# Cached attention decode with a gate: 112-partition weights, ten heads of wo behind the last values, three heads' products moved, a bf16 gate product

## The chip, the cores and the metric

The kernel runs on one core of a Trainium2 chip. The metric is device time in microseconds (us) of the whole launch, the median of three runs. The profile covers the span from the first to the last instruction, which is about 2 us shorter than the device time (2513.1 against 2514.9 us in the profiled run). Five engines matter here: TensorE (PE), VectorE (DVE), ScalarE (ACT), GpSimd (POOL) and SyncE (SP, which only issues transfers), and beside them 16 DMA engines that bring data from HBM into SBUF.

## What is computed

One token is decoded. Its normalised input asks 16 heads of cached keys and values (65,536 positions of 256 numbers each, bf16), and the attention's output is multiplied with a gate that two dense layers make.

```python
x = A_x                                   # 1 x 1 x 448, bf16
xn = _layernorm(x, axis=-1)
q = (xn @ wq)                             # 448 -> 16 heads x 256
scores = einsum("bhqd,bhkd->bhqk", q, k_cache) * (256 ** -0.5)
p = softmax(scores)
o = einsum("bhqk,bhkd->bhqd", p, v_cache) # 16 heads, 65536 keys, 256
s = o.reshape(1, 1, 16 * 256) @ wo        # 4096 -> 448
g = silu(silu(xn @ w1) @ w2)              # 448 -> 1792 -> 448
out = x + s * g
```

Keys and values are 2 x 16 x 65,536 x 256 x 2 bytes, 1,074 MB of the 1,084 MB that the kernel reads. The rest is w1, w2, wq and wo.

## The kernel before: the parts that matter

A head is cut into 4 blocks, so there are 64 blocks of keys and 64 of values. A block is 128 partitions x 128 keys x 256 numbers, 64 KB to a partition. Three buffers `R[0]`, `R[1]`, `R[2]` of that size take keys and values in turn. VectorE and ScalarE share the products of query and keys, TensorE multiplies the softmax's weights with the values (a matmul of 512 columns for two keys), and after the last block the heads' outputs are multiplied with wo ("project", a matmul of 448 columns for half a head).

The first layers' weights lie in `R[2]` until they are used. 448 rows are 3.5 times 128, so each weight comes in two transfers: three rows to a partition, and the last 64 rows cut in halves.

```python
def load_rows(T, M, w, s):
    sp.dma_start(out=T[:, 0 : DF * w],
        in_=M[0 : DF * P].rearrange("(p c) n -> p (c n)", c=DF)).then_inc(s, 16)
    sp.dma_start(out=T[:, DF * w : DF * w + w // 2],
        in_=M[DF * P : D].rearrange("r (z n) -> (r z) n", z=2)).then_inc(s, 16)
# ... the start
    act.dma_start(out=x_f[0:1, :], in_=A_x[0, 0:1, :]).then_inc(dl["x"], 16)
    load_rows(w1_t, B_w1, F, dl["w1"])
    load_rows(wq_t, A_wq, HD, dl["wq"])
    load_keys(R[0], block(Kd, 0), 0, SUB, kl[0])
    # ... w2, the rest of the first key block, the second key block
```

At the end the last values `Vl` come in eight pieces (`vz`, in keys), and wo in pieces of heads (`pieces`). Heads 0 to 2 of wo (`wo_p`, `NPRE = 3`) are loaded early, after the first value block.

```python
    vn = cuts(0, 32, 64, 96, 128)                      # the last but one value block
    vz = cuts(0, 16, 40, 64, 80, 96, 112, 120, 128)    # the last value block
    nz = 2
    pieces = cuts(NPRE, 9, 11, 13, 15, 16)             # wo
# ... the order of the last transfers
    for (k0, k1), w in zip(vn, nl):
        load_keys(R[2], Vn, k0, k1, w)
    take(sp, vf[1])
    for (k0, k1), w in zip(vz[:nz], zl[:nz]):
        load_keys(R[1], Vl, k0, k1, w)
    take(sp, kf[0])
    load_wo(0)
    for (k0, k1), w in zip(vz[nz:], zl[nz:]):
        load_keys(R[1], Vl, k0, k1, w)
    for p in range(1, len(pieces)):
        load_wo(p)
```

TensorE's order at the end, with what ScalarE and VectorE do between (`keys` waits for each piece and multiplies it; `pe_rows` and `pe_bcast` spread a block's maximum; `act_softmax` makes the weights, which `take(pe, pv)` waits for; `pe_turn` turns a block's output):

```python
    keys(psO, 2, 2, vn, nl, 3, 4, False, od)
    act_out(); act_row(LAST - 1)
    take(pe, pv)
    keys(psO2, 0, 1, vz, zl, 0, nz, True)
    need("pe", t_o)
    pe.wait_ge(wp, 16);    project(0, NPRE)
    pe.wait_ge(wl[0], 16); project(*pieces[0])
    pe_turn()
    # ... the third piece, with pe_rows and pe_bcast inside it
    act_softmax(LAST + 1, PV[0][:, HK:KB], HK, KB)
    t_g = silu(g_t, ps_y, g_e, t_y)
    act_out(psO2)
    take(pe, pv)
    t15 = pe_sums(ps_m[:, 0:NL], N1, NENT)
    keys(psO, 0, 1, vz, zl, nz + 1, nz + 2, True)
    pe_turn()
    # ... VectorE: shares and weights of the last head
    keys(psO, 0, 1, vz, zl, nz + 2, len(vz), False, od)
    act_out()
    pe.wait_ge(wl[1], 16); project(*pieces[1])
    t = pe_turn(tok=True)
    # ... VectorE: the last head's output
    for p in range(2, len(pieces) - 1):
        pe.wait_ge(wl[p], 16); project(*pieces[p])
    pe.wait_ge(wl[len(pieces) - 1], 16)
    t = mark("pe", project(H1, H))
    t = mark("dve", dve.tensor_tensor(out=g_t, in0=ps_ao, in1=g_t, op=ALU.mult))
    t = mark("dve", dve.tensor_tensor(out=x_f[0:1, :], in0=g_t, in1=x_f[0:1, :], op=ALU.add))
    sp.dma_start(out=out[0, 0:1, :], in_=x_f[0:1, :]).then_inc(dl["out"], 16)
```

`g_t` and `ps_ao` are fp32, `x_f` is bf16; `ps_ao` lies in PSUM.

Of the kernel before, what the change touches and what calls it, by code (L numbers as in the profile page):

```python
# [14 lines left out]
KB = 128  # L15
# [9 lines left out]
def kernel(  # L25
# [30 lines left out]
    NSTEP = KB // SUB  # L56
    DF = D // P
    assert D == DF * P + P // 2
    HP = H // 2
    DX = DF + 2  # L60
    FC = F // P
# [18 lines left out]
    S = pool.tile([P, KB], fp32, name="S")  # L80
    S2 = pool.tile([P, KB], fp32, name="S2")
    PVV = pool.tile([P, NR * KB], bf16, name="PV")
# [4 lines left out]

    wo_p = pool.tile([P, NPRE, 2 * D], bf16, name="wo_p")
    hist = pool.tile([P, 2 + NENT, 4], fp32, name="hist")
# [6 lines left out]
    sml = pool.tile([P, 16], fp32, name="sml")  # L96
    xnT = pool.tile([P, DX], bf16, name="xnT")
    h1e = pool.tile([P, FC], fp32, name="h1e")
    h1s = pool.tile([P, FC], bf16, name="h1s")
    negM = pool.tile([P, H], fp32, name="negM")  # L100
    cf = pool.tile([P, NENT], fp32, name="cf")
    wgt = pool.tile([P, NENT], fp32, name="wgt")
    tot = pool.tile([P, H], fp32, name="tot")
    part = pool.tile([P, 2, NENT], fp32, name="part")
    OT32 = pool.tile([P, 2, H], fp32, name="OT32")
    OT = pool.tile([P, 2, H], bf16, name="OT")
# [5 lines left out]

    def rest(n0, n):
        return R[2][:, n0 : n0 + n], n0 + n

    wq_t, n = rest(0, DF * HD + HD // 2)
    Z, n = rest(n, DX * HP * HP)
    w1_t, n = rest(n, DF * F + F // 2)
    w2_t, n = rest(n, FC * D)
    xn, n = rest(n, D)  # L120
    xz, n = rest(n, 2 * P)
    h1r, n = rest(n, 2 * F)
    assert n <= KW
    h1r = h1r[0:1, :].bitcast(fp32)
    xn, xz = xn[0:1, :], xz[0:1, :].rearrange("o (z n) -> o z n", z=2)

# [11 lines left out]
    psO2, ps_qh = bank[4][0:2, :], bank[3][0:HP, :]  # L138
    ps_xt, ps_h = bank[2][:, 0:DX], bank[7][:, 0:FC]
    ps_z = bank[6][0:1, D : D + 1]  # L140
# [8 lines left out]
    def mark(e, ins):  # L149
        count[e] += 1  # L150
        ins.then_inc(line[e], 1)
        return (e, count[e])

    def need(e, *toks):
        for p, c in toks:
            if seen.get((e, p), 0) < c:
                eng[e].wait_ge(line[p], c)
                seen[(e, p)] = c
# [4 lines left out]
    def take(e, s, k=1):  # L163
        e.wait_ge(s, k).then_inc(s, -k)  # L164
# [17 lines left out]
    def cuts(*c):  # L182
        return tuple(zip(c[:-1], c[1:]))

    vn = cuts(0, 32, 64, 96, 128)
    vz = cuts(0, 16, 40, 64, 80, 96, 112, 120, 128)
    nz = 2
    nl = [kl[2], kq[2], kh[2], vl[2]]
    zl = [kl[1], kq[1], kh[1], vl[1], vf[2], kf[1], kf[2], sem("zl")]
    pieces = cuts(NPRE, 9, 11, 13, 15, 16)  # L190
    wl = [vf[0], vf[1], vh[2]] + [sem(f"wl{t}") for t in range(3, len(pieces))]
# [28 lines left out]

    def load_rows(T, M, w, s):
        sp.dma_start(
            out=T[:, 0 : DF * w], in_=M[0 : DF * P].rearrange("(p c) n -> p (c n)", c=DF)
        ).then_inc(s, 16)
        sp.dma_start(
            out=T[:, DF * w : DF * w + w // 2],
            in_=M[DF * P : D].rearrange("r (z n) -> (r z) n", z=2),
        ).then_inc(s, 16)

# [107 lines left out]
    def act_out(po=psO):  # L337
        take(act, od)
        act.copy(out=O[:, :], in_=po).then_inc(oc, 1)  # L339

    def act_row(e):
        take(act, ho)
        return act.copy(out=hist[:, at(e + 2), 2:4].rearrange("p o s -> p (o s)"), in_=ps_t)
# [197 lines left out]
    with tc.tile_critical(sync_engine=ET.Pool, no_gpsimd_drain=True):  # L541


        act.dma_start(out=x_f[0:1, :], in_=A_x[0, 0:1, :]).then_inc(dl["x"], 16)
        load_rows(w1_t, B_w1, F, dl["w1"])
        load_rows(wq_t, A_wq, HD, dl["wq"])
        load_keys(R[0], block(Kd, 0), 0, SUB, kl[0])
# [11 lines left out]
        gp.memset(ones_row[:], 1.0)  # L559
        gp.memset(xz, 0.0)  # L560
        gp.memset(ident[:], 0.0)
# [29 lines left out]
        ))  # L591
        need("dve", t, g_c)
        for z in range(2):
            t5 = mark("dve", dve.tensor_copy(
                out=xz[0:1, z, :].rearrange("o (r y) -> o y r", y=2)[:, z, :],
                in_=xn[0:1, DF * P : D],
            ))

        xn_c = xn[0:1, 0 : DF * P].rearrange("o (p c) -> o c p", c=DF)
        need("pe", t5, g_c)  # L600
        for c in range(DX):
            ins = pe.matmul(
                ps_xt[:, c : c + 1],
                lhsT=xn_c[0:1, c, :] if c < DF else xz[0:1, c - DF, :],
                rhs=ones_row[0:1, 0:1],
                start=True,
                stop=True,
            )
# [5 lines left out]
        t_z = mark("dve", dve.tensor_copy(  # L614
            out=Z.rearrange("p (c n) -> p c n", c=DX)[:, :, 0 : (HP - 1) * (HP + 1) + 1 : HP + 1],
            in_=xnT[:, :, None].to_broadcast([P, DX, HP]),
        ))


        def rows(T, w, n0, n1):  # L620
            z, o = (n0 * 2) // w, DF * w
            return [(T[:, c * w + n0 : c * w + n1], c) for c in range(DF)] + [
                (T[:, o + n0 - z * (w // 2) : o + n1 - z * (w // 2)], DF + z)
            ]


        need("pe", t7)
        take(pe, dl["w1"], 32)
        FQ = F // 4
        for g, b in enumerate((0, 1, 5, 6)):  # L630
            for r, (w, c) in enumerate(rows(w1_t, F, g * FQ, (g + 1) * FQ)):
                ins = pe.matmul(
                    bank[b][0:1, 0:FQ],
                    lhsT=xnT[:, c : c + 1],
                    rhs=w,
                    start=(r == 0),
                    stop=(r == DF),
                )
            t = mark("pe", ins)
            need("act", t)  # L640
            t = mark("act", act.copy(out=h1r[:, g * FQ : (g + 1) * FQ], in_=bank[b][0:1, 0:FQ]))
# [21 lines left out]

        take(pe, dl["wq"], 32)
        for r, (w, c) in enumerate(rows(wq_t, HD, 0, Dh)):
            ins = pe.matmul(
                ps_q,
                lhsT=xnT[:, c : c + 1].to_broadcast([P, P]),
                rhs=w,
                start=(r == 0),  # L670
                stop=(r == DF),
            )
        ins.then_inc(qr, 1)
        need("pe", t_z)
        for j in range(HP):
            for r, (w, c) in enumerate(rows(wq_t, HD, j * 2 * Dh, (j + 1) * 2 * Dh)):
                ins = pe.matmul(
                    ps_qh,
                    lhsT=Z[:, (c * HP + j) * HP : (c * HP + j + 1) * HP],
                    rhs=w,  # L680
                    start=(j == 0 and r == 0),
                    stop=(j == HP - 1 and r == DF),
                )
# [173 lines left out]
        def keys(po, t, s, cut, sems, a, b, start, done=None):  # L857
            for n in range(a, b):
                (k0, k1), last = cut[n], n == b - 1
                pe.wait_ge(sems[n], 16)  # L860
                pe_keys(po, t, s, k0, k1, start and n == a, last and done is not None,
                        done if last else None)
# [5 lines left out]
        keys(psO, 2, 2, vn, nl, 3, 4, False, od)  # L868
        act_out()
        act_row(LAST - 1)  # L870


        take(pe, pv)
        keys(psO2, 0, 1, vz, zl, 0, nz, True)
        need("pe", t_o)
        pe.wait_ge(wp, 16)
        project(0, NPRE)
        pe.wait_ge(wl[0], 16)
        project(*pieces[0])
        pe_turn()  # L880
        (k0, k1) = vz[nz]
        assert k1 == HK
        pe.wait_ge(zl[nz], 16)
        pe_keys(psO2, 0, 1, k0, k0 + 8, False, False)
        pe_rows()
        pe_keys(psO2, 0, 1, k0 + 8, k0 + 16, False, False)
        pe_bcast()
        pe_keys(psO2, 0, 1, k0 + 16, k1, False, True, od)
        act_softmax(LAST + 1, PV[0][:, HK:KB], HK, KB)
        t_g = silu(g_t, ps_y, g_e, t_y)  # L890
        act_out(psO2)
        take(pe, pv)
        t15 = pe_sums(ps_m[:, 0:NL], N1, NENT)
        keys(psO, 0, 1, vz, zl, nz + 1, nz + 2, True)
        pe_turn()
        t = mark("dve", shares(N1, NENT, H1, H))
# [8 lines left out]
        outputs(N1, NENT - 1, H1, H, NL - 1)  # L905
        keys(psO, 0, 1, vz, zl, nz + 2, len(vz), False, od)
        act_out()
# [12 lines left out]
        for p in range(2, len(pieces) - 1):  # L920
# [5 lines left out]
        need("dve", t, t_g)  # L926
        t = mark("dve", dve.tensor_tensor(out=g_t, in0=ps_ao, in1=g_t, op=ALU.mult))  # L927
        need("dve", t)
        t = mark("dve", dve.tensor_tensor(  # L929
            out=x_f[0:1, :], in0=g_t, in1=x_f[0:1, :], op=ALU.add  # L930
        ))
        need("sp", t)
# [31 lines left out]
```

## Time and profile before

| what | value |
|---|---|
| time, three runs | 2515.05, 2515.18, 2515.19 us |
| span of the profiled run | 2513.1 us |
| read from HBM | 1084.29 MB, 431 GB/s over the span |
| VectorE busy | 2174.9 us (87%) |
| ScalarE busy | 1930.3 us (77%) |
| TensorE matmul busy | 1148.4 us (46%) |

How to read it: an engine's busy time is the sum of its instructions; a wait is idle time of an engine with what ended it. For the 16 DMA engines the profile has a mean busy share for each stretch, and the trace a record of every packet (its start, duration and size) and of every step by which a transfer's semaphore rises. A transfer of this kernel has landed for its reader when the slowest of its 16 engines is done.

### The profile page before, as it was taken

The numbers are of one execution on the slowest core, as the hardware profiler recorded it, in microseconds if no ns is written. First come the engines' busy times: TensorE is split into PE (matmuls) and PEld (weight loads), VectorE is DVE, ScalarE is ACT, GpSimd is POOL, SyncE is SP. The second block draws the span as 40 slices with busy tenths as digits, with TensorE's granted clock in tenths as the row PEclk, the third lists the DMA queues.
The fourth block names the chain that finished last, engine by engine and source line by source line (L and its number), as shares of the span: only waits on it lengthen the run. The fifth ranks groups of instructions, "written<-read, shape, count | busy, mean of one in ns | idle before, by whom it ended". The sixth has DMA issues, their size and how long they took to land. (4 is left out here: it accounts for less than half of the span.)

```text
span 2513.1 us, 29999 instructions
## 1 busy us (share of the span) xinstructions
PE 1148.4 (46%) x4738; PEld 436.0 (17%) x4738; DVE 2174.9 (87%) x1565; ACT 1930.3 (77%) x9556; POOL 1.9 (0%) x14
## 2 busy tenths in 40 slices
PE   3353543534535445345354353443544534535457
PEld 1121211211112112111121121111211111112123
DVE  6979889889898898898988988989889889898897
ACT  5868778778787787787877877878778778787786
POOL 0000000000000000000000000000000000000000
PEclk7676766767667677677676776776767767677679
DMA  9999999999999999999999999999999999999999
GB/s 426 421 442 434 434 434 433 434 433 432 433 434 434 432 432 432 432 434 433 433 434 434 434 434 434 434 433 434 434 434 434 434 434 434 434 434 434 434 426 375
DMA packets 23464, 1084.37 MB, mean 431 GB/s; under 512 B 2466, under 2 KB 4644, under 8 KB 5028
## 3 DMA queue, kind: packets, MB, share of 16 engines
q1 hardware_dynamic: 23458, 1084.30, 99.9%
q8 instruction: 4, 0.07, 0.0%
q10 hardware_dynamic: 2, 0.00, 0.0%
HBM read 1084.29 MB, written 0.00 MB: 431 GB/s over the span
## 5 line engine op out<-in xcount | busy, mean ns | idle before, releaser
L313 ACT ACTIVATE R<-R x4608 | 1839.0, 400 | 368.6 <-ACTq L164 368.6
L250 DVE TENSOR_TENSOR R<-R,qcur 128x4608 bf16<-128x4608 bf16 (+1 forms) x512 | 1131.1, 2220 | 248.7 <-DVEq L164 248.6
L348 PE MATMUL bank<-R,PV 128*2 128x512 bf16 x4096 | 1028.8, 418 | 18.7 <-PEq L164 6.0
L296 DVE TENSOR_REDUCE S<-R 128x13 f32<-128x3328 bf16 (+1 forms) x256 | 926.0, 3617 | 0.0
L313 ACT ACTIVATION_READ_ACCUMULATOR R<-R x4608 | 858.2, 186 | 0.0
L348 PEld LDWEIGHTS bank<-R,PV 128*2 128x2 bf16 x4096 | 365.0, 90 | 652.6 <-issue 212.5
L360 PE MATMUL bank<-ident,rmax 128*1 128x128 bf16 x65 | 17.0, 262 | 931.4 <-PEq L164 931.4
L377 PE MATMUL bank<-eye,O 2*128 2x2 f32 x264 | 40.1, 253 | 378.7 <-PEq L164 378.7
L360 PEld LDWEIGHTS bank<-ident,rmax 128*1 128x1 bf16 x65 | 5.1, 79 | 936.0 <-issue 935.9
L326 ACT ACTIVATE hist<-bank 128x1 f32 (+1 forms) x65 | 11.1, 171 | 158.0 <-ACTq L164 158.0
L284 DVE CUSTOM_DVE_ANT_0 R<-R,qcur 128x256 bf16<-128x256 bf16 x252 | 105.5, 419 | 0.0
L377 PEld LDWEIGHTS bank<-eye,O 2*128 2x128 f32 x264 | 36.3, 206 | 396.4 <-issue 396.4
L232 DVE TENSOR_REDUCE gmax<-bank 1x1 bf16<-1x128 f32 x65 | 18.3, 281 | 37.1 <-DVEq L164 37.1
L339 ACT COPY O<-bank 2x512 f32<-2x512 f32 x67 | 37.5, 559 | 8.2 <-ACTq L164 8.2
L271 DVE CAST qcur<-bank 128x256 bf16<-128x256 f32 x64 | 27.2, 425 | 16.0 <-DVEq L164 15.9
L328 ACT ACTIVATE PV<-S,hist 128x128 f32 (+1 forms) x65 | 26.0, 400 | 14.7 <-ACTq L164 14.5
L391 PE MATMUL bank<-q,ident 8*128 (+1 forms) x63 | 24.3, 386 | 7.8 <-issue 1.4
L243 DVE COPY S<-S 128x128 f32<-128x128 f32 (+1 forms) x65 | 14.7, 226 | 11.7 <-DVEq L164 2.5
L284 DVE DVE_READ_ACCUMULATOR2_ANT S<- 128x1 f32 x252 | 20.9, 83 | 0.0
L244 DVE TENSOR_REDUCE rmax<-S 128x1 bf16<-128x128 f32 (+1 forms) x65 | 18.2, 279 | 0.0
L366 PE MATMUL bank<-gmax,ones_row 1*128 1x1 bf16 x65 | 10.4, 159 | 4.4 <-PEq L164 0.6
L328 ACT ACTIVATION_READ_ACCUMULATOR PV<-S,hist (+1 forms) x65 | 12.1, 186 | 0.0
(72 smaller groups left out, 98.7 us busy)
## 6 DMA issues: line engine op xcount, KB each, us to landing
R<-in_A_k_cache_dram SPq DMA_DIRECT2D x7, 4096.0 KB, 26.4
R<-in_A_v_cache_dram SPq DMA_DIRECT2D x4, 2048.0 KB, 17.1
R<-in_A_k_cache_dram SPq DMA_DIRECT2D x2, 2048.0 KB, 19.3
R<-in_A_v_cache_dram SPq DMA_DIRECT2D x4, 1024.0 KB, 18.9
R<-in_A_wq_dram SPq DMA_DIRECT2D x1, 3072.0 KB, 12.9
R<-in_A_v_cache_dram SPq DMA_DIRECT2D x2, 1536.0 KB, 21.7
R<-in_B_w_dram SPq DMA_DIRECT2D x1, 1568.0 KB, 24.7
R<-in_B_w_dram SPq DMA_DIRECT2D x1, 1344.0 KB, 5.9
```

What stands on the lines that cost most here:

```text
L232: dve.reduce_max(out=gmax[0:1, :], in_=ps_m[0:1, :], axis=AX.X).then_inc(gm, 1)
L250: return dve.tensor_tensor(out=keys, in0=keys, in1=qcur[:, None, :].to_broadcast([P, c1 - c0, Dh]), op=ALU.mult,)
L271: dve.tensor_copy(out=qcur[:, :], in_=ps_q).then_inc(sd, 1)
L284: dve.tensor_tensor_reduce(out=Kv[:, c, :], in0=Kv[:, c, :], in1=qcur[:, :], scale=1.0, scalar=0.0, op0=ALU.mult, op1=ALU.add, accum_out=S ...
L296: ins = dve.tensor_reduce(out=S[:, c1:c2], in_=Kv[:, c1:c2, :], axis=AX.X, op=ALU.add)
L313: ins = act.activation(out=prod, in_=prod, func=ACT.Identity, accum_out=S[:, bass.ds(c0 + c, 1)],)
L328: act.activation(out=pv_out, in_=S2[:, c0:c1], func=ACT.Exp, bias=col(0, 1), scale=scale, accum_out=col(1, 2),).then_inc(pv, 1)
L339: act.copy(out=O[:, :], in_=po).then_inc(oc, 1)
L348: ins = pe.matmul(po, lhsT=PV[t][:, c : c + 2], rhs=R[s][:, c * Dh : (c + 2) * Dh], start=(start and c == k0), stop=(stop and c == k1 - 2),)
L360: pe.matmul(ps_m[0:1, :], lhsT=rmax[:, 0:1], rhs=ident[:, :], start=True, stop=True).then_inc(tm, 1)
L377: ins = pe.matmul(ps_t2[:, 2 * a : 2 * a + 2], lhsT=Ov[:, j, a, :], rhs=eye2[:, j, :], start=(j == 0), stop=(j == 1), is_transpose=True,)
L391: pe.matmul(ps_q, lhsT=ident[0:HP, at(j)].to_broadcast([HP, P]), rhs=q8[:, o : o + Dh] if isinstance(o, int) else q8[:, bass.ds(o, Dh)], s ...
```

## The change

The change has four parts. The first layers' weights w1 and wq come in one transfer each, four rows to a partition on 112 partitions, so that the two half-row transfers, the zero-padded copies of the input and the split index go away. The order of the end is changed: three pieces of Vl (64 keys) come ahead of wo's first piece, which is now three heads, and ten heads of wo come behind the last values, in six pieces. TensorE multiplies wo's first three heads ahead of its wait for the last softmax weights. And the product with the gate is written as bf16, so that the last addition reads two bf16 operands. The smaller tiles S2, cf, wgt, part and OT32 share one tile with wo_p, in whose place the hidden layer's row stands at the start; that makes the room.

```diff
-    DF = D // P
-    assert D == DF * P + P // 2
+    DC = 4
+    PD = D // DC
+    assert PD * DC == D and PD <= P and PD % 16 == 0
...
-    def load_rows(T, M, w, s):
-        sp.dma_start(
-            out=T[:, 0 : DF * w], in_=M[0 : DF * P].rearrange("(p c) n -> p (c n)", c=DF)
-        ).then_inc(s, 16)
-        sp.dma_start(
-            out=T[:, DF * w : DF * w + w // 2],
-            in_=M[DF * P : D].rearrange("r (z n) -> (r z) n", z=2),
-        ).then_inc(s, 16)
+    def load_rows(T, M, s):
+        sp.dma_start(out=T, in_=M.rearrange("(p c) n -> p (c n)", c=DC)).then_inc(s, 16)
...
-        load_rows(w1_t, B_w1, F, dl["w1"])
-        load_rows(wq_t, A_wq, HD, dl["wq"])
+        load_rows(w1_t, B_w1, dl["w1"])
+        load_rows(wq_t, A_wq, dl["wq"])
...
-    nz = 2
+    nz = 3
...
-    pieces = cuts(NPRE, 9, 11, 13, 15, 16)
+    pieces = cuts(NPRE, 6, 8, 10, 12, 14, 15, 16)
...
-        act_out()
-        act_row(LAST - 1)
-
-        take(pe, pv)
-        keys(psO2, 0, 1, vz, zl, 0, nz, True)
         need("pe", t_o)
         pe.wait_ge(wp, 16)
         project(0, NPRE)
+        take(pe, pv)
+        keys(psO2, 0, 1, vz, zl, 0, nz, True, od)
+        act_out()
+        act_softmax(LAST + 1, PV[0][:, HK:KB], HK, KB)
+        act_row(LAST - 1)
+        act_out(psO2)
+        pe_rows()
         pe.wait_ge(wl[0], 16)
         project(*pieces[0])
+        pe_bcast()
         pe_turn()
-        (k0, k1) = vz[nz]
...
-        act_softmax(LAST + 1, PV[0][:, HK:KB], HK, KB)
         t_g = silu(g_t, ps_y, g_e, t_y)
-        act_out(psO2)
         take(pe, pv)
+        keys(psO, 0, 1, vz, zl, nz, nz + 1, True)
+        pe_turn()
         t15 = pe_sums(ps_m[:, 0:NL], N1, NENT)
-        keys(psO, 0, 1, vz, zl, nz + 1, nz + 2, True)
-        pe_turn()
...
-        keys(psO, 0, 1, vz, zl, nz + 2, len(vz), False, od)
+        keys(psO, 0, 1, vz, zl, nz + 1, len(vz), False, od)
...
-        t = mark("dve", dve.tensor_tensor(out=g_t, in0=ps_ao, in1=g_t, op=ALU.mult))
+        sg = q8[0:1, 0:D]
+        t = mark("dve", dve.tensor_tensor(out=sg, in0=ps_ao, in1=g_t, op=ALU.mult))
         need("dve", t)
-        t = mark("dve", dve.tensor_tensor(
-            out=x_f[0:1, :], in0=g_t, in1=x_f[0:1, :], op=ALU.add
-        ))
+        t = mark("dve", dve.tensor_tensor(out=x_f[0:1, :], in0=sg, in1=x_f[0:1, :], op=ALU.add))
```

More of the change, by code (lines that the diff above doesn't have):

```diff
@@ L56 @@
     NSTEP = KB // SUB
-    DF = D // P
-    assert D == DF * P + P // 2
+    DC = 4
+    PD = D // DC
+    assert PD * DC == D and PD <= P and PD % 16 == 0
     HP = H // 2
-    DX = DF + 2
     FC = F // P
@@ L80 @@
     S = pool.tile([P, KB], fp32, name="S")
-    S2 = pool.tile([P, KB], fp32, name="S2")
     PVV = pool.tile([P, NR * KB], bf16, name="PV")
@@ L86 @@
     O = pool.tile([2, 2 * Dh], fp32, name="O")
-    wo_p = pool.tile([P, NPRE, 2 * D], bf16, name="wo_p")
+    early = pool.tile([P, 2 * F], bf16, name="early")
     hist = pool.tile([P, 2 + NENT, 4], fp32, name="hist")
@@ L96 @@
     sml = pool.tile([P, 16], fp32, name="sml")
-    xnT = pool.tile([P, DX], bf16, name="xnT")
+    xnT = pool.tile([PD, DC], bf16, name="xnT")
     h1e = pool.tile([P, FC], fp32, name="h1e")
@@ L100 @@
     negM = pool.tile([P, H], fp32, name="negM")
-    cf = pool.tile([P, NENT], fp32, name="cf")
-    wgt = pool.tile([P, NENT], fp32, name="wgt")
     tot = pool.tile([P, H], fp32, name="tot")
-    part = pool.tile([P, 2, NENT], fp32, name="part")
-    OT32 = pool.tile([P, 2, H], fp32, name="OT32")
     OT = pool.tile([P, 2, H], bf16, name="OT")
@@ L110, with share @@
     eps_t, rstd = sml[0:1, 12:13], sml[0:1, 13:14]
[L113 to L125, printed above, removed]
+    def share(n0, T, *counts):
+        for c in counts:
+            yield T[:, n0 : n0 + c]
+            n0 += c
+        assert n0 <= T.shape[1]
+    wq_t, Z, w1_t, w2_t, xn = share(0, R[2], DC * HD, DC * HP * HP, DC * F, FC * D, D)
+    wq_t, Z, w1_t, xn = wq_t[0:PD, :], Z[0:PD, :], w1_t[0:PD, :], xn[0:1, :]
+    h1r = early[0:1, :].bitcast(fp32)
+    wo_p, *late = share(0, early, NPRE * 2 * D, *(2 * n for n in (KB, NENT, NENT, 2 * NENT, 2 * H)))
+    wo_p = wo_p.rearrange("p (h e) -> p h e", h=NPRE)
+    S2, cf, wgt, part, OT32 = (T.bitcast(fp32) for T in late)
+    part, OT32 = (T.rearrange("p (a n) -> p a n", a=2) for T in (part, OT32))
     WW = NHA * D
@@ L138 @@
     psO2, ps_qh = bank[4][0:2, :], bank[3][0:HP, :]
-    ps_xt, ps_h = bank[2][:, 0:DX], bank[7][:, 0:FC]
+    ps_xt, ps_h = bank[2][0:PD, 0:DC], bank[7][:, 0:FC]
     ps_z = bank[6][0:1, D : D + 1]
@@ L186 @@
     vz = cuts(0, 16, 40, 64, 80, 96, 112, 120, 128)
-    nz = 2
+    nz = 3
+    assert vz[nz - 1][1] == HK
     nl = [kl[2], kq[2], kh[2], vl[2]]
     zl = [kl[1], kq[1], kh[1], vl[1], vf[2], kf[1], kf[2], sem("zl")]
-    pieces = cuts(NPRE, 9, 11, 13, 15, 16)
+    pieces = cuts(NPRE, 6, 8, 10, 12, 14, 15, 16)
     wl = [vf[0], vf[1], vh[2]] + [sem(f"wl{t}") for t in range(3, len(pieces))]
@@ L559 @@
         gp.memset(ones_row[:], 1.0)
-        gp.memset(xz, 0.0)
         gp.memset(ident[:], 0.0)
@@ L591 @@
         ))
[L592 to L596, printed above, removed]
-            ))
-        xn_c = xn[0:1, 0 : DF * P].rearrange("o (p c) -> o c p", c=DF)
-        need("pe", t5, g_c)
-        for c in range(DX):
+        xn_c = xn.rearrange("o (p c) -> o c p", c=DC)
+        need("pe", t, g_c)
+        for c in range(DC):
             ins = pe.matmul(
                 ps_xt[:, c : c + 1],
-                lhsT=xn_c[0:1, c, :] if c < DF else xz[0:1, c - DF, :],
+                lhsT=xn_c[0:1, c, :],
                 rhs=ones_row[0:1, 0:1],
@@ L614 @@
         t_z = mark("dve", dve.tensor_copy(
-            out=Z.rearrange("p (c n) -> p c n", c=DX)[:, :, 0 : (HP - 1) * (HP + 1) + 1 : HP + 1],
-            in_=xnT[:, :, None].to_broadcast([P, DX, HP]),
+            out=Z.rearrange("p (c n) -> p c n", c=DC)[:, :, 0 : (HP - 1) * (HP + 1) + 1 : HP + 1],
+            in_=xnT[:, :, None].to_broadcast([PD, DC, HP]),
         ))
         def rows(T, w, n0, n1):
[L621 to L624, printed above, removed]
+            return [(T[:, c * w + n0 : c * w + n1], c) for c in range(DC)]
         need("pe", t7)
-        take(pe, dl["w1"], 32)
+        take(pe, dl["w1"], 16)
         FQ = F // 4
@@ L636 @@
                     start=(r == 0),
-                    stop=(r == DF),
+                    stop=(r == DC - 1),
                 )
@@ L662 @@
         t_h = silu(h1s[:, :], ps_h, h1e[:, :], t)
-        take(pe, dl["wq"], 32)
+        take(pe, dl["wq"], 16)
         for r, (w, c) in enumerate(rows(wq_t, HD, 0, Dh)):
@@ L667 @@
                 ps_q,
-                lhsT=xnT[:, c : c + 1].to_broadcast([P, P]),
+                lhsT=xnT[:, c : c + 1].to_broadcast([PD, P]),
                 rhs=w,
                 start=(r == 0),
-                stop=(r == DF),
+                stop=(r == DC - 1),
             )
@@ L681 @@
                     start=(j == 0 and r == 0),
-                    stop=(j == HP - 1 and r == DF),
+                    stop=(j == HP - 1 and r == DC - 1),
                 )
@@ L877 @@
         project(0, NPRE)
+        take(pe, pv)
[5 more added lines that the diff above has]
+        pe_rows()
         pe.wait_ge(wl[0], 16)
         project(*pieces[0])
+        pe_bcast()
         pe_turn()
-        (k0, k1) = vz[nz]
[L882 to L888, printed above, removed]
-        act_softmax(LAST + 1, PV[0][:, HK:KB], HK, KB)
         t_g = silu(g_t, ps_y, g_e, t_y)
-        act_out(psO2)
         take(pe, pv)
+        keys(psO, 0, 1, vz, zl, nz, nz + 1, True)
+        pe_turn()
         t15 = pe_sums(ps_m[:, 0:NL], N1, NENT)
-        keys(psO, 0, 1, vz, zl, nz + 1, nz + 2, True)
-        pe_turn()
         t = mark("dve", shares(N1, NENT, H1, H))
@@ L926 @@
         need("dve", t, t_g)
-        t = mark("dve", dve.tensor_tensor(out=g_t, in0=ps_ao, in1=g_t, op=ALU.mult))
+        sg = q8[0:1, 0:D]
+        t = mark("dve", dve.tensor_tensor(out=sg, in0=ps_ao, in1=g_t, op=ALU.mult))
         need("dve", t)
-        t = mark("dve", dve.tensor_tensor(
-            out=x_f[0:1, :], in0=g_t, in1=x_f[0:1, :], op=ALU.add
-        ))
+        t = mark("dve", dve.tensor_tensor(out=x_f[0:1, :], in0=sg, in1=x_f[0:1, :], op=ALU.add))
         need("sp", t)
```

## The prediction

> **What bounds the kernel now.** I read the page first: the 40 slices, then the chain that ended last.
>
> ```profile
> DMA  9999999999999999999999999999999999999999
> GB/s 426 421 442 434 434 434 433 434 433 432 433 434 434 432 432 432 432 434 433 433 434 434 434 434 434 434 433 434 434 434 434 434 434 434 434 434 434 434 426 375
> HBM read 1084.29 MB, written 0.00 MB: 431 GB/s over the span
> ```
>
> The DMA engines are full in every slice. Only the first two and the last two slices (62.8 us each) move less than 434 GB/s. 1084.29 MB at 434 GB/s are 2498 us, so some 15 us of the 2513.1 are start and end, and nothing done to an engine in the middle can count. The packet records say it more sharply: from the ramp's end near 3 us until past 2506 us at least 16 packets are in flight at practically every moment. The 15,616 packets of 65,536 B take 2422 ns in the median, 27.06 GB/s for each DMA engine. So a DMA engine that falls behind at the start has no pause in which to catch up. The landings show this too: a code fetch at 65 us delays one engine, the third key block lands between 77.32 and 79.06 us, engine by engine, and at the end the last piece still lands between 2506.77 and 2508.34.
>
> The chain in order of time ends so (start us, us, what):
>
> ```profile
> 2487.21 20.64 DMA R<-in_A_wo_dram
> 2507.86 0.04 issue
> 2507.90 1.31 PE bank L840 x6
> 2509.21 0.02 issue
> 2509.23 0.62 DVE R L927
> 2509.86 0.02 issue
> 2509.88 0.61 DVE x_f L929
> ```
>
> The reader is to see that six products with wo run after a landing, although the last piece holds one head, two products. The piece of heads 13 and 14 lands at 2507.86, its four products run, and the last two follow, whose weights came at 2508.34 while the four ran. Then two VectorE operations and the output's transfer. TensorE at the end (start us, us, engine, line, operation, in brackets the idle time before):
>
> ```profile
> 2480.84 3.61 PE L348 MATMUL bank<-R,PV 128*2 128x512 bf16 x16 [0.42 <-DMA R<-in_A_v_cache_dram]
> 2485.72 4.48 PE L348 MATMUL bank<-R,PV 128*2 128x512 bf16 x20 [1.26 <-PEq L164]
> 2490.03 1.30 PE L840 MATMUL bank<-wo_p,OT 128*1 128x448 bf16 x6
> 2491.17 2.43 PE L840 MATMUL bank<-R,OT 128*1 128x448 bf16 x12
> ...
> 2500.00 5.36 PE L348 MATMUL bank<-R,PV 128*2 128x512 bf16 x24
> 2505.51 0.92 PE L840 MATMUL bank<-R,OT 128*1 128x448 bf16 x4
> 2506.36 0.63 PE L377 MATMUL bank<-eye,O 2*128 2x2 f32 x4
> 2506.92 2.27 PE L840 MATMUL bank<-R,OT 128*1 128x448 bf16 x10
> ```
>
> TensorE waits 1.26 us for the last softmax (its weights are ready at 2485.6) and is then almost without a pause until 2509.2. By start times a product of 448 columns costs 0.189 us, one of 512 columns 0.215 us.
>
> [...] L250 in bf16 takes 1.88 us for 3328 elements and 2.55 for 4608, 0.52 ns each; the fp32 products L927 and L929 take 0.61 us for 448.
>
> **The change part by part.**
>
> *bf16 product.* L927 reads PSUM and fp32 and stays at 0.61 us. L929 then reads two bf16 rows: from the two L250 sizes the fixed part is 1.88 - 3328 x 0.000523 = 0.14 us, and 448 x 0.000523 + 0.14 = 0.37. On the path: -0.24 us.
>
> *Three heads in the pause.* Six products, 6 x 0.189 = 1.13 us, fit between 2484.29 and 2485.6, so the wait for the softmax ends as before. This gives TensorE 1.13 us later. It loses some again: Vl's third piece now follows the second directly and lands at 2486.97 + 3.69 = 2490.66 (3.69 is the spacing of the 24-key pieces), while TensorE would want it at 2490.02: 0.65 us of waiting. Then, with ScalarE free at 2492.93 as before, I get: maximum and three heads until 2494.8, weights ready about 2496.0, a wait of 0.4 us; fourth piece until 2497.8; turn and sums until 2498.8; 24 products of values until 2503.9; heads 6 and 7 until 2504.7; the turn at 2504.9, after ScalarE's copy; heads 8 to 11 until 2507.0.
>
> *Ten heads behind the values.* Bytes and their total do not change, so the last landing stays at 2508.34 apart from the start. Counting back 0.60 us for each head (2505.47 to 2506.67 for two), heads 12 and 13 land at 2507.27, head 14 at 2507.86. TensorE reaches them at 2507.0, 0.3 us early. From 2507.31 eight products take 8 x 0.189 = 1.51 us, end 2508.82; from the last landing two products would end at 2508.76. Before, the same end was 2507.90 + 6 x 0.189 = 2509.03. So -0.21 us: the end remains bound by landings.
>
> *112 partitions.* Per engine before: 8 x (10,752 + 1,792 + 24,576 + 4,096 B), by the intervals between packets 8 x (0.401 + 0.071 + 0.909 + 0.156) = 12.30 us. After, if each engine keeps its rate: 7 x (14,336 + 32,768 B), interpolated between packet sizes 7 x (0.535 + 1.213) = 12.24, and two semaphore writes fewer: -0.1 us. That is what the part is for. [...] at 27.06 GB/s the 47.1 KB more are +1.74 us[...]. The queue stays full to the end, so this lag would last. [...] First packets of 14,336 B in place of 10,752 may win back up to 0.3 us in the ramp. This part's sum is the doubtful one: -0.1 to +5, and I take +1.6 as its middle.
>
> Work of the first layers (L632 to L692) ends at 34 us, and buffer R[2] is wanted by the queue only near 57: what they gain or lose is hidden. Sum: 2515.18 - 0.24 - 0.21 + 1.6 = 2516.3 us.
>
> **The rivals.** First, *ports do not bind*: the engines do, at 27.06 GB/s each, and the first part is worth -0.1; then 2514.6. [...] Second, *engines collide*: +2 to +5 us, 2517 to 2519.8. [...] Against it: several packets in flight may smooth it. [...] Third, *TensorE becomes the bound*: my 0.3 us of slack before heads 12 and 13 is small; 0.5 us more of waiting on the softmax weights near 2496 would put back 0.2 us. [...] Fourth, *code fetches*: four fetches of 16 KB (65.0, 2434.9, 2446.7, 2489.6 us) share the DMA engines; the one at 65 us makes the following packet 0.46 us longer and itself takes 1 us. The end comes when the latest engine ends, so a second fetch on an engine already late adds up to 1 us, and none on a late one takes as much away. Nothing in the change steers that.
>
> **Range and chances.** Ports not binding 2514.6 (one in five), ports alone about 2516.3, collisions up to 2519.8. I predict 2516.3 us, 2514.3 to 2519.8 for 8 in 10. Even the ends of the range are within 0.2% of before: faster by 2% 0.003, within 2% 0.99, slower by 2% 0.007.
>
> **What would show it.** Landings of w1 and wq: before, wq lands between 14.07 and 14.71 us over its 16 engines; with full ports the latest is 1.5 us or more later and the spread wider, and the same lag stands in the spread of every landing up to the last one. Packets of 14,336 and 32,768 B then take longer at the start than 0.54 and 1.22 us. If the packets keep these, the ports do not bind and the last landing is at 2508.2. At the end: L929's successor at 0.37 us, six products with wo ahead of the pause's end, eight after the landing of heads 12 and 13. The prediction is wrong in its largest term if the packets of the start keep their rate, and wrong in its small ones if TensorE comes to heads 12 and 13 after they landed.

## The result

The changed kernel takes 2522.23 us (median of six runs, 2521.55 to 2523.71), the kernel before 2515.18 (six runs, 2515.05 to 2515.32). The ratio is 1.0029, 95% interval 1.0016 to 1.0042: 7 us slower, which is small and clear. The prediction was 2516.3 us with 2514.3 to 2519.8 as its range, so the time lies outside it.

From the page of the changed kernel, the 40 slices:

```profile
DMA  9999999999999999999999999999999999999999
GB/s 366 431 438 433 433 433 433 433 433 433 434 433 433 436 435 437 433 435 435 435 433 433 433 433 433 433 433 433 433 433 433 434 433 434 436 436 435 433 427 377
HBM read 1084.29 MB, written 0.00 MB: 430 GB/s over the span
```

All 40 slices still say "DMA full". The first slice alone is different: 366 GB/s where it was 426. 60 GB/s less over a slice of 63 us are 3.8 MB, and 3.8 MB at 434 GB/s are 8.7 us. The DMA share is the time that packets take, and packets that take longer fill it as well (0.96 with 229 GB/s from 8 to 12 us below, 0.95 with 412 before), so the row of nines does not show a loss that the row under it does.

Stretches of 4 us, from 4 us on, show where. Columns: stretch, its length, then the busy time and number of instructions of PE, PE's weight loads, DVE, ACT and POOL, the granted clock, DMA share, GB/s. Before:

```profile
4.00:8.00 4.00, 0.78 (x7) 0.45 (x8) 1.54 (x8) 0.53 (x2) 0.00 (x0) 1.00 1.09 456
8.00:12.00 4.00, 4.00 (x13) 1.34 (x11) 0.00 (x0) 1.04 (x2) 0.00 (x0) 1.00 0.95 412
12.00:16.00 4.00, 2.83 (x19) 1.95 (x17) 0.26 (x2) 2.51 (x4) 0.00 (x0) 0.97 1.03 436
16.00:20.00 4.00, 3.89 (x13) 1.41 (x14) 0.75 (x3) 0.00 (x0) 0.00 (x0) 0.61 0.98 422
20.00:24.00 4.00, 4.00 (x20) 1.65 (x19) 3.00 (x2) 0.00 (x0) 0.00 (x0) 1.00 1.00 430
```

Changed:

```profile
4.00:8.00 4.00, 0.57 (x4) 0.49 (x4) 0.93 (x4) 0.23 (x1) 0.00 (x0) 1.00 1.28 362
8.00:12.00 4.00, 2.17 (x6) 0.75 (x7) 0.00 (x0) 0.48 (x1) 0.00 (x0) 1.00 0.96 229
12.00:16.00 4.00, 3.97 (x11) 1.15 (x9) 0.00 (x0) 1.09 (x3) 0.00 (x0) 1.00 0.92 262
16.00:20.00 4.00, 1.77 (x14) 1.69 (x14) 0.59 (x3) 1.99 (x3) 0.00 (x0) 0.92 1.04 279
20.00:24.00 4.00, 0.48 (x3) 0.39 (x4) 0.00 (x0) 0.00 (x0) 0.00 (x0) 0.50 0.77 233
24.00:28.00 4.00, 4.00 (x12) 1.18 (x11) 0.43 (x1) 0.00 (x0) 0.00 (x0) 0.50 1.01 430
```

From 8 to 24 us, while w1 and wq come in, 229 to 279 GB/s flow, at a DMA share of 0.92 to 1.04 until 20 us and 0.77 in the last stretch; once the key blocks have followed, on 128 partitions, it is 430 again. The packet records agree: packets of 32,768 B of wq take 2.09 us in the median, where such packets of keys take 1.21, and w1's of 14,336 B take 0.755 in the median, where 0.535 is what the fastest take.

The end, in order of time, from the chain of the changed kernel:

```profile
2512.98 0.60 PE bank L368 x4
2513.59 3.25 PE bank L819 x16
2516.84 0.02 issue
2516.86 0.62 DVE q L899
2517.48 0.02 issue
2517.51 0.38 DVE x_f L901
```

L899 and L901 are the product with the gate and the last addition. The addition takes 0.38 us where it took 0.61. Sixteen products run without a break and end just after the last landing (2516.23 us). TensorE around the moved products:

```profile
2492.19 1.30 PE L819 MATMUL bank<-early,OT 128*1 128x448 bf16 x6
2493.62 4.48 PE L339 MATMUL bank<-R,PV 128*2 128x512 bf16 x20
2498.66 2.75 PE L339 MATMUL bank<-R,PV 128*2 128x512 bf16 x12 [0.56 <-DMA R<-in_A_v_cache_dram]
...
2504.11 1.89 PE L339 MATMUL bank<-R,PV 128*2 128x512 bf16 x8 [0.52 <-PEq L160]
```

The six products fill the old pause of 1.26 us; two shorter waits are new, 0.56 us for Vl's third piece and 0.52 for the last softmax weights, as foreseen.

The sum, by landings of the slowest of 16 engines:

```
                                   before    changed   difference
w1 landed                            7.38       9.70      +2.32
wq landed                           15.97      23.38      +7.41
keys 0 to 31 landed                 20.86      28.18      +7.32
last piece of wo landed           2508.34    2516.23      +7.89
end of the span                    2513.1     2520.5      +7.4
```

Before, w1 and wq come in two transfers each, and the second one's landing is taken. So +7.3 us are lost by the time the first keys are in and never come back; +0.6 arise on the way to the last landing, and -0.5 is the shorter end (4.27 us after the last landing where it was 4.76).

### The profile page after: what moved, and what is told of

It reads as the page before. It is cut to its first block, busy times and chain, and to the rows that moved or that the text cites. A ratio compares the mean times of both kernels' runs of the same rounds, so it can differ in the third digit from the quotient of the medians.

```text
span 2520.5 us, 29993 instructions
## 1 busy us (share of the span) xinstructions
PE 1147.0 (46%) x4737; PEld 436.6 (17%) x4737; DVE 2174.2 (86%) x1563; ACT 1930.0 (77%) x9556; POOL 1.6 (0%) x13
## 5 line engine op out<-in xcount | busy, mean ns | idle before, releaser
L319 ACT ACTIVATE PV<-early,hist 128x128 f32 (+1 forms) x65 | 26.0, 400 | 14.7 <-ACTq L160 14.4
L234 DVE COPY early<-S 128x128 f32<-128x128 f32 (+1 forms) x65 | 14.7, 226 | 9.6 <-DVEq L160 0.2
L665 ACT CAST q<-bank 8x512 bf16<-8x512 f32 x1 | 0.6, 576 | 15.5 <-PE bank L656 15.5
```

The lines of the kernel that those rows point to most:

```text
L319: act.activation(out=pv_out, in_=S2[:, c0:c1], func=ACT.Exp, bias=col(0, 1), scale=scale, accum_out=col(1, 2),).then_inc(pv, 1)
```

## The experiments

Theory A: packets to 112 partitions are slow because of the partitions that they write, and the full queue keeps what is lost. Rival B: the larger packets, or the addresses they are read from, are slow. Rival C: the new order of the end costs the time. A "port", in the prediction and the expectations, is an assumption of the author's: a way into SBUF that some partitions share. No trace shows one; the runs show times for sets of partitions. Times are medians; the kernel before, timed again beside each group of versions, stood at 2515.2 to 2515.3 us.

**Which part.** First the loads on 128 partitions again, all else changed:

```diff
-    load_rows(w1_t, B_w1, dl["w1"])       # 112 partitions, 4 rows each
+    load_rows(w1_t, B_w1, F, dl["w1"])    # 128 partitions, 3 rows each, and the halves
```

(and the same for wq, with the zero-padded copies and the split index of before; the shared tile stays).

> The changed kernel with one part undone: w1 and wq come on 128 partitions again, in two transfers each. Theory A [...]: wq's last landing is back near 14.7 us and the time is 2514.7 us, that is 2515.18 less 0.24 (bf16 operands) and 0.21 to 0.26 (order of the end). Rival C (the new order of the end costs time): 2521 to 2522 us, with wq at 14.7 all the same.

Measured: 2514.73 us (12 runs, 2514.59 to 2515.64), ratio 0.9998, interval 0.9989 to 1.0007. C is out, A or B stands. wq landed at 15.82 us; the expected 14.7 was the landing of the first of its two transfers, which came at 14.54. The chain ends so:

```profile
2489.35 18.05 DMA R<-in_A_wo_dram
2507.40 0.04 issue
2507.45 1.69 PE bank L839 x8
2509.14 0.02 issue
2509.16 0.62 DVE q L919
2509.78 0.02 issue
2509.80 0.38 DVE x_f L921
```

That is the end as the prediction had it: heads 12 and 13 land at 2507.40 (predicted 2507.27), eight products follow, then two VectorE operations, the second shorter.

The other way round, the 112 partitions alone, with the order of the end, the pieces and the product of before (the two values that differ are shown, the order is as above in the kernel before):

```diff
-    nz = 3
-    pieces = cuts(NPRE, 6, 8, 10, 12, 14, 15, 16)
+    nz = 2
+    pieces = cuts(NPRE, 9, 11, 13, 15, 16)
```

> The 112-partition loads alone: order of the end, pieces of wo and the fp32 product are as before. Theory A: 2522.2 + 0.5 = 2522.7 us, wq's last landing near 23.4 us. Rival C: 2515.2 us.

Measured: 2522.61 us (seven runs), ratio 1.0029, interval 1.0018 to 1.0041; wq landed at 23.26 us. The loads carry the whole loss.

Then one weight at a time on 112 partitions (w1: `load_rows` in the new form, wq in the old; and the reverse).

> The changed kernel with w1 alone on 112 partitions, wq on 128 in two transfers. w1 has 1.6 of the 5.3 MB. Theory A, with the loss shared by bytes: 30% of 7.3 us, 2.2 us over the version with both on 128 partitions, 2516.9 us. If only packets of 32 KB lose (rival B, packet size or source address), it stays at 2514.7.

> The changed kernel with wq alone on 112 partitions, w1 on 128. Theory A: 70% of 7.3 us, 5.1 us over the version with both on 128, 2519.8 us. Together with the run for w1 the two losses should sum to that of the change, 7.3 us; if they don't, the two transfers make each other slow.

Measured: 2516.97 us for w1 alone (+2.24 over 2514.73) and 2521.10 for wq alone (+6.37). w1 loses what its bytes say. wq loses more than its share, 6.4 in place of 5.1, and the two sum to 8.6, more than the change's 7.5. The expectation of a plain sum was wrong: wq lost less behind a w1 on 112 partitions (23.38 - 9.70 = 13.7 us between the landings of w1 and wq) than behind a w1 on 128 (22.99 - 7.50 = 15.5). Why is not shown.

**Partitions or packets.** Packets of the changed kernel's size, on all partitions:

```diff
-    sp.dma_start(out=T, in_=M.rearrange("(p c) n -> p (c n)", c=DC)).then_inc(s, 16)
+    src = bass.AP(M.tensor, M.offset, [[3 * w, P], [1, DC * w]])   # rows 3p .. 3p+3
+    sp.dma_start(out=T, in_=src).then_inc(s, 16)
```

> The changed kernel's packets (14,336 and 32,768 B, four consecutive rows of the weights to a partition) on all 128 partitions: partition p takes rows 3p to 3p+3, so the rows overlap, 8/7 of the bytes move, and the first layers multiply other rows than they should. Theory A (ports): [...] packets keep 0.54 and 1.22 us, and 8 x (0.535 + 1.213) = 13.98 us in place of 12.30 give 2514.7 + 1.7 = 2516.4 us. Rival B (the size of the packets or their source addresses make them slow): packets of 0.75 and 2.1 us as in the changed kernel, 2523 us or more.

Measured: 2516.33 us. Packets of 32,768 B of wq took 1.213 us, nearly all of them. The first stretches (columns as above):

```profile
4.00:8.00 4.00, 0.61 (x5) 0.56 (x6) 0.93 (x4) 0.23 (x1) 0.00 (x0) 1.00 1.04 441
8.00:12.00 4.00, 4.00 (x11) 1.30 (x12) 0.00 (x0) 1.04 (x2) 0.00 (x0) 1.00 1.04 451
12.00:16.00 4.00, 3.26 (x20) 2.11 (x18) 0.00 (x0) 2.42 (x4) 0.00 (x0) 1.00 1.04 451
```

More bytes than the change moves, in packets of the same size from the same matrix, at 441 to 451 GB/s. And the other half of the test, the same partitions with other packets and addresses, row c*112 + p on partition p:

```diff
-    sp.dma_start(out=T, in_=M.rearrange("(p c) n -> p (c n)", c=DC)).then_inc(s, 16)
+    sp.dma_start(out=T.rearrange("p (c n) -> p c n", c=DC),
+                 in_=M.rearrange("(c p) n -> p c n", c=DC)).then_inc(s, 16)
```

> The changed kernel with the same 112 partitions as target, but row c*112 + p on partition p, so that a packet is one row (3,584 and 8,192 B) and the source addresses are others. Theory A: as slow as the changed kernel, 2521 to 2524 us. Rival B: 2514.7 to 2515.5 us.

Measured: 2521.97 us, wq landed at 22.43 to 25.51. The partitions decide, not the packets: B is out.

**Which partitions.** Here transfers of 16 partitions are used, so that it is known which a transfer writes together. Slices of 16 consecutive partitions:

```diff
-    sp.dma_start(out=T, in_=M.rearrange("(p c) n -> p (c n)", c=DC)).then_inc(s, 16)
+    M3 = M.rearrange("(p c) n -> p (c n)", c=DC)
+    for j in range(7):
+        sp.dma_start(out=T[16*j : 16*(j+1), :], in_=M3[16*j : 16*(j+1)]).then_inc(s, 16)
```

> Each weight in seven transfers of 16 consecutive partitions[...]. Theory A, [...] 2514.7 + 36.5 = 2551 us. Rival B: near 2522 us or less, since packets and sources are those of the changed kernel.

Measured: 2546.78 us (two runs), 32 us over 2514.73 and 4 us under the 2551 expected. wq's packets took 4.55 us, nearly all of them, where 1.21 is the time on 128 partitions: 16 packets at once have 16 x 32,768 B / 4.548 us = 115 GB/s together. In stretches of 4 us from 4 to 28 us this run moved 115 to 163 GB/s. The 36.5 us of the expectation rested on an assumption about which partitions share a way in, which no run shows.

Slices with a step of 7 (`T[j : 112 : 7]`):

> Each weight in seven transfers, the j-th to partitions j, j+7, ... j+105[...]. If the 112-partition transfer deals consecutive rows to each engine, this is the same traffic: wq lands near 22 to 23.4 us, time near 2522 us. If it deals rows in another way, the landings differ clearly; if traffic in 14 transfers costs in itself, it is slower.

Measured: 2523.16 us, 0.9 us over the changed kernel's median and inside the spread of its runs. The last 16 landing steps of wq came at 22.24 to 24.63 us, the latest 1.25 us after the changed kernel's; packets of wq took 2.07 us in the median (2.09 in the changed kernel). The change's transfer behaves much like these slices; whether it deals seven consecutive rows to each engine is not shown, since no record names the engine.

Slices with a step of 8 (`T[j : 128 : 8]`, eight of them):

> Each weight in eight transfers of 16 partitions, the j-th to partitions j, j+8, ... j+120[...]. The eighth transfer repeats rows, so 8/7 of the bytes move, as in the run on 128 overlapping partitions, and the first layers multiply other rows than they should. [...] the start takes twice the 13.98 us, 2516.3 + 12 to 14 = 2528.5 to 2530.5 us, packets of 32,768 B take 2.2 to 2.4 us. Measured with steps of 7, [...] these packets already took up to 2.2 us for all engines[...].

Measured: 2530.84 us (two runs), packets of 32,768 B 2.56 us in the median, 2.1 times the 1.21 on 128 partitions. So the time of a packet follows which 16 partitions are written together: 4.55 us for consecutive ones, 2.56 with a step of 8, 2.07 with a step of 7. With a step of 7 the mean was 1.99 us, and all sixteen landing steps came nearly alike: the next landing, the first key piece, came at 27.93 to 29.30 us. Why one set is slower than another is not shown.

**Who waits.** Eight partitions more heavily loaded, on the version with loads on 128 partitions: 262 KB more, from ScalarE's queue, to partitions 0-3 and 32-35; and as a control the same bytes to all partitions. The later transfer of these bytes waits for them. In theory S everything waits, in theory L only what goes to these partitions.

```diff
+    for p in (0, 32):
+        act.dma_start(out=R[1][p : p + 4, h0:KW],
+                      in_=block(Kd, 1)[p : p + 4, h0:KW]).then_inc(xs, 16)
```

> The version with loads on 128 partitions, and two more transfers of 4 partitions each (0-3 and 32-35, [...] 32 KB to a partition, 262 KB in all, bytes that a later transfer brings again) from ScalarE's queue at the start. Each runs on 4 engines. Theory S (waiting spreads): all 16 engines are late at the first half of the second key block, by several us, as with 112 partitions. Theory L [...]: at least 12 of the 16 semaphore steps of the later landings come as without the extra (those of the first key pieces at 19.9 to 20.7 and 24.8 to 25.6 us), and up to 4 are late, by up to 262 KB / 27.06 GB/s = 9.7 us. The time is 2514.7 + up to 9.7 us in both.

> The control to the run before: the same 262 KB more, as one transfer of 2 KB to each of 128 partitions. Every engine and port gets 16.4 KB more, 0.6 us at 27.06 GB/s (0.65 with packets of 2 KB): all 16 landings of the key pieces 0.6 to 0.7 us later, 2515.4 us, in both theories.

Measured: 2523.40 and 2515.58 us. The 16 landing steps of the first key piece:

```
loads on 128 partitions    19.90 .. 20.72   (all 16)
same bytes on 128          20.93 .. 21.47   (all 16)
eight partitions loaded    26.66 .. 27.16   (12 of 16), 29.71, 29.92, 30.11, 30.50
```

262 KB to eight partitions hold up all 16 landing steps. The two extra transfers raised their semaphore in four landing steps each. Twelve steps of the key piece are 6.4 to 6.8 us late all the same, and four are 9.8 late; that these four are of the engines with the extra is not shown, since the steps do not name their engine. The first stretches of that run:

```profile
4.00:8.00 4.00, 0.29 (x5) 0.21 (x5) 1.26 (x6) 0.53 (x2) 0.00 (x0) 1.00 1.46 338
8.00:12.00 4.00, 0.00 (x0) 0.00 (x0) 0.00 (x0) 0.00 (x0) 0.00 (x0) 1.00 0.87 127
12.00:16.00 4.00, 0.00 (x0) 0.00 (x0) 0.00 (x0) 0.00 (x0) 0.00 (x0) 1.00 0.82 160
16.00:20.00 4.00, 2.88 (x8) 1.00 (x9) 0.00 (x0) 0.52 (x1) 0.00 (x0) 1.00 0.94 402
```

While the extra transfers run (they land by 16.5 us), the whole core gets 127 to 160 GB/s, then 402. Nor do the engines run out of work: from 8 to 15.5 us there are 15 to 18 packets in flight at every moment, 16.1 in the mean, as many as there are engines, and the first twelve packets of wq take 2.8 to 3.5 us each, where packets of this size (24,576 B) take 0.91. Each holds the rows of one partition, so at least four of them to others than the eight: the packets themselves are slow, those to other partitions too. The control's landings are 0.8 to 1.0 us late, a little more than the expected 0.6 to 0.7. What makes the packets beside the loaded partitions slow is not seen in the trace, and no run loads another set of eight. The extra rows are also read from other addresses than the control's, so the source side has no control of its own in this pair; the runs with overlapping and with single rows above are what speaks against it.

**The small parts.** On the version with loads on 128 partitions, the fp32 product alone put back (`out=g_t` in place of `out=sg`), the end alone put back, and a variant of the end with four heads ahead of the fourth value piece and nine behind:

```diff
-    pieces = cuts(NPRE, 6, 8, 10, 12, 14, 15, 16)
+    pieces = cuts(NPRE, 7, 9, 11, 13, 14, 15, 16)
...
     pe_turn()
+    project(NPRE + 3, pieces[0][1])
```

> Loads on 128 partitions and the new order of the end, but the product with the gate written in fp32 as before. If the bf16 product is worth what the row of the last addition shows (0.61 to 0.38 us), this is 2514.73 + 0.23 = 2514.96 us.

> Loads on 128 partitions and the bf16 product, but order of the end and pieces of wo as before. If the new order is worth 0.2 us, this is 2514.95 us; if it is worth nothing, 2514.73.

> Loads on 128 partitions, bf16 product, and four heads of wo ahead of the fourth piece of values (the fourth head's two products run where TensorE waits 0.52 us for the last softmax weights), nine behind, the last four heads of wo one by one. The end is bound by landings: heads 12 and 13 land at 2507.40 and eight products follow now; one by one the last two products after the last landing bind. Expected -0.06 us against 2514.73, so 2514.67; if TensorE and not the landings bound the end, -0.38.

Measured: 2515.01, 2514.98 and 2514.70 us, 13 runs each. Against 2514.73 the bf16 product is worth 0.28 us and the order of the end 0.25. The variant gains 0.03, nothing that can be told from zero. Single runs of one version spread over up to 1 us, each of the three ratios to before has an interval of about 0.999 to 1.001 that holds 1, and 2514.73 comes from another group of runs, in which the kernel before was 0.05 us faster; the medians fall where expected, but it is the traces that carry these two readings. For the product it is the row of the addition, 0.38 us in place of 0.61. For the order it is the end of the chain with the old order:

```profile
2508.07 0.04 issue
2508.11 1.31 PE bank L838 x6
2509.42 0.02 issue
2509.45 0.62 DVE q L926
```

The last landing is at 2508.56 us here and at 2508.53 with the new order, but the product with the gate starts at 2509.45 in place of 2509.16, 0.29 us later. Each is one execution.

## Why the prediction was wrong

*What bounds the kernel* held, and decided the outcome: the queue is full from 3 us on, so a loss at the start stays. The first key piece was 7.3 us late, the last landing 7.9. (One reading in it is loose: it says that only four slices move less than 434 GB/s, while eleven between them show 432 or 433. The 36 between average 433.8, so its 15 us for start and end stand.)

*bf16 product*, predicted -0.24: the addition took 0.38 us, as worked out (0.37). Right.

*Three heads in the pause* and *ten heads behind the values*, predicted -0.21: measured -0.25 by the medians, -0.29 in the traces, with the predicted wait of 0.65 us for the third piece at 0.56 and that of 0.4 us for the weights at 0.52. In the version on 128 partitions the chain runs through the landing of heads 12 and 13 and eight products, as predicted. In the changed kernel itself TensorE came to these heads just as they landed, without the 0.3 us of slack, and the chain names TensorE; it cost nothing that could be measured. Right.

*112 partitions* is the step that failed: "-0.1 to +5, and I take +1.6 as its middle". That the loss would come from the partitions was right; how it arises is not shown. The term measured +7.5 us (2522.23 - 2514.73), above the end of its range. Two things in it were mis-sized. The +1.74 is the time of 47.1 KB, eight rows of the new lengths in place of eight of the old, at the 27.06 GB/s of packets at full rate; that eight rows bound a load which has seven to an engine in the mean (112 for 16) was the author's assumption. The run with 128 overlapping rows has eight of the new rows to an engine in the mean and wq's packets at 1.213 us, and it costs about this: 2516.33 - 2514.73 = 1.6 us. In the changed kernel the packets themselves became slow, 2.09 us, which the +1.74 leaves out; it was made the middle all the same. And the upper end, +5, was a guess for the latest engine alone, with the others going on. The run with eight loaded partitions shows otherwise: all sixteen landing steps are 6.4 us late and more. So what had to be estimated was a loss of all sixteen, and the estimate for one was too low. That waiting of this kind makes up the rest, the 5.9 us over the 1.6, is argued from that run and not shown. The sentence "several packets in flight may smooth it", set against this rival, pointed the wrong way.

Of the rivals, *ports do not bind* (one in five) is out in what it foresaw, packets that keep their rate: they took 2.09 us in place of 1.21; *engines collide* came nearest, and the time lies beyond its 2519.8, but that engines collide is not shown; *TensorE becomes the bound* came true in name only. *Code fetches*: again four, now at 108.5, 2442.5, 2454.7 and 2497.1 us. The spread over the 16 engines was 0.78 us at the first key piece (0.61 before) and 1.89 at the last landing (1.57 before), so the wider spread makes 0.15 of the 0.6 us by which the delay grew between them. What makes the rest, and what a fetch has to do with it, was not tried.

The predicted signs were all there: wq later by more than 1.5 us (7.4) and more spread (0.63 us before, 1.40 after; the 14.07 to 14.71 us of the prediction were the first of wq's two transfers, the second landed from 15.34 to 15.97), packets at 0.755 and 2.09 us in place of 0.54 and 1.22, the same lag to the end.

The best versions are those with the loads on 128 partitions and the rest of the change, 2514.73 and 2514.70 us, half a microsecond under before in the median, with an interval that still holds no difference.

## What to carry to other kernels

In a kernel bound by transfers, time each large load on the partitions that it will use, beside the same packets on all 128; a tidy layout on 112 partitions cost here 7.5 us where its longer packets were to save 0.1. Read GB/s beside the DMA share: packets that take longer fill it as well, so a share of 0.96 with 229 GB/s, where 430 flow elsewhere, is a queue that waits. And when some partitions are overloaded, do not estimate the loss from the transfers to these alone before a run has shown that the others go on; here all 16 landing steps of the next piece were 6.4 us late and more.

## What the runs showed that was not expected

262 KB more on eight partitions made all 16 landing steps at least 6.4 us late, the same bytes on 128 partitions 0.8 to 1.0. Packets of 32,768 B to 16 partitions took 4.55 us where the partitions were consecutive, 2.56 with a step of 8 and 2.07 with a step of 7, where they take 1.21 on 128. And the changed kernel's runs spread over 2.2 us (2521.55 to 2523.71) where the kernel before spread over 0.3 in as many runs; but in 16 to 33 later runs it spread over 0.9 to 1.3 as well, so it is not shown that the change is what spreads them.
